# Attention and a gated product on one core: the gate's filter taps, the planner's orders and the split between plain and split matmuls

## The chip, the cores and the metric

The kernel runs on one core of one Trainium2 chip. The metric is the device time of one execution in microseconds (us), the median over runs. A core has five instruction streams here: TensorE (PE, with its weight loads shown as PEld), VectorE (DVE), ScalarE (ACT), GpSimd (POOL), and SyncE (SP), whose queue issues most transfers.

## What is computed

```
B, H, S, D = 8, 12, 448, 64;  DM = 768;  KT = 5
scores = q @ k.T / sqrt(D) - log(S)
attn   = sigmoid(scores)                      # 8 x 12 heads, 448 x 448
x      = attn @ v                             # gathered to (8, 448, 768)
gate   = sigmoid(sum over k of conv_w[k] * x delayed by KT-1-k tokens)   # 5 taps for each channel
out    = (gate * (x @ w_val)) @ w_out
```

Everything is float32 at the interface.

## The kernel before

**Tiles.** Two heads of one batch make a pair: 48 pairs i, six for each batch. Two pairs make a step j, so there are 24 steps, three for each batch. For each pair TensorE makes three chunks of 128 keys of the transposed scores (`scores`, L516), for each step one more accumulator with the remaining 64 keys of both pairs (`scores_rest`, L539), and then the product of the sigmoids with v (`attend`, L602 and L610). All of these use a ring of three PSUM accumulators, `ps_a`. The last step of each batch completes x for 448 tokens. Batch 0's x is written to DRAM and comes back in slices of 64 tokens, one slice behind each of the batches 1 to 7, so the later part works on 7 groups of 512 tokens. For each group, `product` (L753) makes six column blocks of x @ w_val and six of the gated value @ w_out, 18 matmuls of 512 columns each, in a ring of two PSUM accumulators, `ps_m`.

**Two ways to multiply.** A float32 operand can be taken plain, or be split into a high and a low part that are multiplied in three products. `WHOLE` names the steps whose attention product is plain (j from 0 to 7, that is 16 pairs), `WHOLE_SCORES` the pairs whose scores are plain (i from 0 to 14). A plain step needs only a sigmoid on ScalarE for each chunk (`attention`, L552, tile a_single). A split step needs the sigmoid, a scaling on ScalarE (L367, a<-ps_a) and a subtraction on VectorE (L563) for each of its seven accumulators, a maximum over v on VectorE (L531), a one-column matmul for it (L536), four small exponent instructions (L544 to L577) and the two parts of v (L369 or L367, and L583). A split pair needs qk_hi (L361 or L363) and qk_lo, two subtractions on GpSimd (L372).

**The gate.** In `after(j)`, for the groups 1 to 7 (21 steps): x is copied out of PSUM, its maximum taken (L658), and then for each of the step's two channel blocks the first tap is one scaled copy into the gate (L367 or L369). Of the other four taps, the first one or two are multiply-adds on VectorE (L679); the last two (group 1, `ADDED_FIRST`) or three (groups 2 to 7, `ADDED`) are multiplied on ScalarE into a `tap` tile (L367) and added to the gate in memory by a transfer that GpSimd issues (L683). A sigmoid over both blocks follows (L685). The gate is read when a value product leaves PSUM (L777, the tile y), and y then gives the two parts of the operand g of the second product.

**Scale of x.** `x_largest` (L696 to L702) spreads the group's largest |x| over the partitions by two small matmuls, which ride in front of the first chunk of a later pair's scores; `x_scale` and `x_split` then make xs, the operand of the value products.

**Weights.** Each of the twelve column blocks of w_val and w_out is loaded as 64-bit words (L410, a ring of three `words` tiles), converted by a few bit operations (`convert`, L387 to L389, L369 or L367, L412), its maximum taken (L415), and split (L446).

**The order.** No loop of the kernel is the order of the instructions. Each operation is entered in a `Plan` with its engines and modelled costs, a priority, and what it depends on. `issue` runs an event model once and picks for each free engine the ready operation of the lowest priority number. The priorities come from hand-set offsets (`AT`) added to the modelled time `tau` of a pair. An engine then executes its instructions strictly in that order. In the model GpSimd and VectorE don't run at the same time where both operations name "VG" as their port.

Of the kernel before, what the change touches and what calls it, by code (L numbers as in the profile page):

```python
# [10 lines left out]
F32 = mybir.dt.float32  # L11
# [4 lines left out]
U32 = mybir.dt.uint32  # L16
I16 = mybir.dt.int16
I64 = mybir.dt.int64
AF = mybir.ActivationFunctionType
ALU = mybir.AluOpType  # L20
# [18 lines left out]
WHOLE = {*range(8)}  # L39
WHOLE_SCORES = {*range(15)}  # L40
# [15 lines left out]
REBIAS = 2.0**-112  # L56
WN = NC * P
# [5 lines left out]
WORDS = 3  # L63
# [10 lines left out]
ADDED_FIRST = 2  # L74
ADDED = 3
# [3 lines left out]
    first=6.63, step=13.72, val=-77.5, val_step=60.94, out=57.5, out_step=597.15, w_max=-57.5,  # L79
    w_split=-155, load_qk_first=-152, load_qk=69.5, load_v=-40.5, split_hi=-2, split_lo=30,  # L80
    rest_first=95.5, rest=251, a_first=-174.5, a=-7, attend=-47.5, v_max=76.5, v_exp=14.5,
    v_split=-159.5, x=-174.5, x_max=-98, x_scale=-307, x_hi=52.5, x_lo=-185.5, x_step=2940.66, tap=51,
    scores=68.5, a_rest=85, a_rest_first=-72.5, tap_first=22, tap_pair=68.5, tap_step=56.18, gate=-110,
    product=63.5, y=-61.5, g_hi=186.5, g_lo=6, o=-97, share=0.3, w_load=-117,
# [39 lines left out]
class Op:  # L124
    __slots__ = ("ways", "prio", "emit", "deps", "n", "start", "end", "eng", "after", "size", "port", "then")
# [7 lines left out]
class Plan:  # L133
# [45 lines left out]
    def issue(self):  # L179
# [24 lines left out]
        while events:  # L204
# [6 lines left out]
            for e in engines:  # L211
# [24 lines left out]
                if o.size:  # L236
                    bus = max(bus, t + cost) + o.size / self.DMA_RATE
                    o.end = bus + self.DMA_DELAY
                else:
                    o.end = t + cost  # L240
# [3 lines left out]
                for x in nexts[o.n]:  # L244
                    same = e in x.ways and len(x.ways) == 1 and not o.size
                    release(x, o.end + (0.03 if same else self.HOP[e]))
# [6 lines left out]
        return order  # L253


@with_exitstack
def attention_then_gate(
# [51 lines left out]
    gate_ring = ring(sb, 4, [P, 2, T], F32, "gate")  # L309
# [9 lines left out]
    tap_ring = ring(sb, 2, [P, 2, T], F32, "tap")  # L319
# [61 lines left out]
    def convert(w, t, prio, c):  # L381

        low, high = (lambda: w()[:, :, 0]), (lambda: w()[:, :, 1])
        part = lambda n: w().bitcast(I16)[:, :, n]
        op({"V": 0.06 + 0.41 * c}, prio, lambda e: nc.vector.tensor_scalar(  # L387
            low(), low().bitcast(U32), 2.0**-29, 7.0, op0=ALU.mult, op1=ALU.min), [], [t])
        op({"V": 0.06 + 0.76 * c}, prio + 0.1, lambda e: nc.vector.tensor_scalar(  # L389
            part(1), part(3), -0x8000, None, op0=ALU.bitwise_and), [], [t])  # L390
        op({"A": 0.06 + 0.76 * c, "V": 0.06 + 0.41 * c}, prio + 0.2, lambda e: scaled(
            e, high().bitcast(F32), high().bitcast(F32), REBIAS), [], [t])

# [235 lines left out]
    def after(j):  # L629
# [34 lines left out]
        g, at, added = gate_ring.new(), t + AT["tap"], ADDED_FIRST if f == 1 else ADDED  # L664
        for p in range(2):
            st[2 * j + p]["g"] = g
        parts = [lambda p=p: by(g()[:, p, :]) for p in range(2)]
        w = lambda p, k: cw()[:, 2 * c + p, KT - 1 - k : KT - k]
        for p, part in enumerate(parts):
            op({"A": 0.61, "V": 0.41}, at + AT["tap_pair"] * p, lambda e, p=p, part=part: scaled(  # L670
                e, part(), x()[:, p, :, HALO:], w(p, 0)), [x, own, cw], [g])
        for k in range(1, KT):
            tap = tap_ring.new() if k > KT - 1 - added else None
            for p, part in enumerate(parts):
                if tap:
                    op({"A": 0.61}, at + AT["tap_step"] * k - AT["tap_first"] + AT["tap_pair"] * p, lambda e, p=p, k=k, tap=tap: scaled(
                        e, by(tap()[:, p, :]), x()[:, p, :, HALO - k : HALO + SL - k], w(p, k)), [x, own, edge, cw], [tap])
                else:
                    op({"V": 0.67}, at + AT["tap_step"] * k + AT["tap_pair"] * p, lambda e, p=p, part=part, k=k: nc.vector.scalar_tensor_tensor(  # L679
                        part(), x()[:, p, :, HALO - k : HALO + SL - k], w(p, k), part(), op0=ALU.mult, op1=ALU.add),  # L680
                       [x, own, edge, cw], [g])
            if tap:
                op({"G": 1.1}, at + AT["tap_step"] * k, lambda e, tap=tap: nc.gpsimd.dma_start(  # L683
                    g(), tap(), accum_op=ALU.add), [tap], [g], 4 * P * T * 4, "")
        op({"A": 0.95}, t + AT["gate"], lambda e: nc.scalar.activation(g(), g(), AF.Sigmoid), [], [g])  # L685
# [52 lines left out]
    def product(n, b, m):  # L738
# [34 lines left out]
        if n == "val":  # L773
# [4 lines left out]
                y(), po(), y_scale()[:, m : m + 1], gate()[:, m % 2, :], op0=ALU.mult, op1=ALU.mult), [po, gate, y_scale], [y], port="")  # L778
# [38 lines left out]
    def score(i, after=None, sums=(), then=()):  # L817
        first, middle, last = (scores(i, c, sums if c == 0 else ()) for c in range(3))
# [4 lines left out]
        for f in then:  # L823
            f(st[i]["ps", 0])
# [14 lines left out]
    for j in range(TWOS):  # L839
# [18 lines left out]
        if j + 1 < TWOS:  # L858
# [12 lines left out]
            score(2 * j + 3, None, sums, then)  # L871
# [76 lines left out]
```

## Time and profile before

| | us |
|---|---|
| median of 3 runs (578.79 to 579.93) | 579.44 |
| the profiled execution | 579.76 |
| its span, first to last instruction | 578.0 |
| PE busy | 571.4 |
| DVE busy | 428.4 |
| ACT busy | 435.4 |
| POOL busy | 138.2 |

The profile is one execution. Busy time of an engine counts a stretch once where two of its instructions overlap. The time of an execution is the span plus what lies around it, here 1.76 us.

### The profile page before, as it was taken

Reading aid. Unit: us, or ns where it says so; the run is one execution under the profiler, and the core shown is the slowest. Engines: PE = TensorE matmul, PEld = TensorE weight load, DVE = VectorE, ACT = ScalarE, POOL = GpSimd, SP = SyncE. Lnnn points to the kernel's source line nnn. Section 1 sums busy time; section 2 is a strip of 40 time slices with the busy share of each in tenths; the row PEclk is TensorE's granted clock in tenths of the full one; section 3 lists DMA queues with packets and bytes.
Section 4 is the critical chain, followed back from the end, with each engine's and each line's share of the span. In section 5 each row is a group of like instructions: output and inputs, shape, how many; then the busy total and the mean of one; then the engine's idle time right before and its main releaser. Section 6 shows DMA issues by size and latency. Waiting matters only on the chain.

```text
span 578.0 us, 9459 instructions
## 1 busy us (share of the span) xinstructions
PE 571.4 (99%) x3592; PEld 280.2 (48%) x3592; DVE 428.4 (74%) x693; ACT 435.4 (75%) x579; POOL 138.2 (24%) x162
## 2 busy tenths in 40 slices
PE   9999999999999999999999999999999999999997
PEld 5343334455555555545555454554545555544444
DVE  1867999899977959888598886889777886760310
ACT  5677988879888869778697878788788897862112
POOL 0000203332424222243322333223322322110000
PEclk9999999999999999999999999999999999999999
DMA  8988677757484564825657364565635663355012
GB/s 327 355 279 267 174 210 188 203 120 184 124 215 83 146 157 141 207 58 155 136 158 176 102 169 96 166 156 155 169 74 168 155 133 74 72 128 129 2 37 74
DMA packets 39310, 88.44 MB, mean 153 GB/s; under 512 B 14944, under 2 KB 20448, under 8 KB 39264
## 3 DMA queue, kind: packets, MB, share of 16 engines
q0 software_dynamic: 8640, 31.46, 29.4%
q1 hardware_dynamic: 30624, 56.37, 28.9%
q8 instruction: 28, 0.46, 0.3%
q14 instruction: 18, 0.15, 0.1%
HBM read 43.96 MB, written 12.40 MB: 98 GB/s over the span
## 4 chain that ended last, share of the span: by engine, by line
PE 90%; DVE 5%; ACT 3%; DMA 1%; issue 1%; ACTq 0%; DVEq 0%
PE ps_m L753 54%; PE ps_a L516 15%; PE ps_a L610 14%; PE ps_a L539 3%; PE ps_a L602 2%; DMA gate<-tap 1%; ACT a_single L552 1%; DVE x_max L658 1%; DVE gate L679 1%; PE ps_m L800 1%; DVE a L563 1%; DVE w_words L389 1%; DVE out_max L415 0%; ACT tap L367 0%; ACT a L367 0%
## 5 line engine op out<-in xcount | busy, mean ns | idle before, releaser
L753 PE MATMUL ps_m<-g,w_out_hi 128*128 128x512 f16 (+1 forms) x516 | 150.5, 374 | 0.0
L753 PE MATMUL ps_m<-xs,w_val_hi 128*128 128x512 f16 x504 | 150.1, 379 | 0.0
L552 ACT ACTIVATE ps_a<-ps_a 128x896 f32<-128x896 f32 x112 | 99.3, 909 | 14.2 <-DVE v_exp L544 6.5
L563 DVE SCALAR_TENSOR_TENSOR a<-ps_a,a 128x896 f16<-128x896 f32 x96 | 100.8, 1082 | 7.0 <-ACT a L367 6.7
L372 POOL TENSOR_TENSOR qk_lo<-qk_src,qk_hi 128x448 fp32r<-128x448 f32 x66 | 75.2, 1151 | 119.8 <-ACT qk_hi L361 36.7
L753 PE MATMUL ps_m<-g,w_out_lo 128*128 128x512 f16 (+1 forms) x258 | 96.5, 374 | 0.0
L683 POOL DMA_DIRECT2D gate<-tap x60 | 53.5, 892 | 178.6 <-ACT tap L367 70.2
L753 PE MATMUL ps_m<-xs,w_val_lo 128*128 128x512 f16 x252 | 95.5, 379 | 0.0
L367 ACT ACTIVATE a<-ps_a 128x896 f16<-128x896 f32 x96 | 85.0, 927 | 0.2
L367 ACT ACTIVATE tap<-x,cw 128x512 f32<-128x512 f32 x120 | 82.2, 739 | 1.5 <-DMA gate<-tap 1.5
L753 PEld LDWEIGHTS <-w_out_hi 128*128 128x128 f16 x516 | 49.0, 98 | 59.6 <-issue 5.3
L753 PEld LDWEIGHTS <-w_val_hi 128*128 128x128 f16 x504 | 47.8, 98 | 61.1 <-issue 5.9
L777 DVE SCALAR_TENSOR_TENSOR y<-ps_m,y_scale,gate 128x512 f32<-128x512 f32 x42 | 29.9, 745 | 34.3 <-PE ps_m L753 34.3
L610 PE MATMUL ps_a<-a,v_hi 128*64 128x448 f16 x384 | 52.7, 354 | 0.0
L367 ACT ACTIVATE y<-ps_m,o_scale 128x512 f32<-128x512 f32 (+1 forms) x35 | 23.1, 678 | 38.0 <-PE ps_m L753 25.4
L552 ACT ACTIVATE a_single<-ps_a 128x896 f32<-128x896 f32 x56 | 48.0, 927 | 4.5 <-PE ps_a L516 4.1
L361 ACT CAST g<-y 128x512 f16<-128x512 f32 x28 | 17.2, 618 | 33.7 <-DVE y L777 32.9
L516 PE MATMUL ps_a<-qk_hi 64*128 64x448 f32 x198 | 39.8, 398 | 0.1
L753 PEld LDWEIGHTS <-w_out_lo 128*128 128x128 f16 x258 | 25.2, 98 | 29.2
L753 PEld LDWEIGHTS <-w_val_lo 128*128 128x128 f16 x252 | 24.7, 98 | 29.7
L516 PE MATMUL ps_a<-qk_single 64*128 64x448 f32 x180 | 39.0, 566 | 0.0
L610 PE MATMUL ps_a<-a_single,v_src 128*64 128x448 f32 x192 | 37.8, 543 | 0.0
(108 smaller groups left out, 752.9 us busy)
## 6 DMA issues: line engine op xcount, KB each, us to landing
gate<-tap POOLq DMA_DIRECT2D x60, 512.0 KB, 4.9
qk_src<-qk SPq DMA_DIRECT2D x33, 448.0 KB, 5.4
v_src<-vs SPq DMA_DIRECT2D x24, 448.0 KB, 4.3
out_t<-y SPq DMA_DIRECT2D x41, 224.0 KB, 3.1
qk_single<-qk SPq DMA_DIRECT2D x15, 448.0 KB, 5.9
w_words<-w_val SPq DMA_DIRECT2D x6, 768.0 KB, 8.1
w_words<-w_out SPq DMA_DIRECT2D x6, 768.0 KB, 5.4
x<-first_x SPq DMA_DIRECT2D x21, 68.0 KB, 4.2
```

The costliest lines, as they stand in the source:

```text
L361: nc.scalar.copy(to, x)
L367: nc.scalar.activation(to, x, AF.Copy, scale=by)
L372: engines[eng].tensor_tensor(to, x, y, op=ALU.subtract)
L516: mm(b()[:, h, :S], k()[rows, at : at + P], q()[rows, :S], start=(n == 0), stop=(n == len(terms(i)) - 1))
L539: mm(b()[to, h, :S], x[n]()[rows, CW:], x[n]()[rows, :S], start=True, stop=True)
L552: nc.scalar.activation(to, b()[:, :, :S], AF.Sigmoid, bias=-math.log(S), scale=1.0 / math.sqrt(D))
L563: op({"V": 1.0}, t + 0.5, lambda e: nc.vector.scalar_tensor_tensor(part(1), p(), A_SCALE, part(0), op0=ALU.mult, op1=ALU.subtract), [b], [ ...
L602: mm(px()[to, p, :S], v()[rows, h * D : (h + 1) * D], x(s["a"])[rows, h, at : at + S], start=(j > 0 and n == 0), stop=(j == 0 and n == len ...
L610: mm(px()[to, p, :S], v()[:, o : o + D], x(st[2 * j + p]["a", c])[:, h, at : at + S], start=(j == 0 and c == 0 and n == 0), stop=(j > 0 an ...
L683: op({"G": 1.1}, at + AT["tap_step"] * k, lambda e, tap=tap: nc.gpsimd.dma_start(g(), tap(), accum_op=ALU.add), [tap], [g], 4 * P * T * 4, "")
L753: mm(po()[:, cs], w()[:, c, :], x(k)[:, cs], start=(c == 0 and j == 0), stop=(c == NC - 1 and j == 2))
L777: op({"V": 0.66}, t + AT["y"], lambda e: nc.vector.scalar_tensor_tensor(y(), po(), y_scale()[:, m : m + 1], gate()[:, m % 2, :], op0=ALU.m ...
```

## The change

All four later taps become multiply-adds on VectorE, the `tap` tiles and the adding transfers go, and the gate is one tile for each channel block, each with a sigmoid of its own. `WHOLE` loses step 7 (14 pairs remain), `WHOLE_SCORES` pair 14. The ring of weight words has four tiles for three. The first bit operation of a weight's conversion may also go to ScalarE. For step 5 the spreading matmuls ride in front of the third chunk of a pair's scores, not the first. `issue` makes the order four times: after each, `deadlines` walks the order backward from the times at which TensorE's operations would run without a gap and gives every operation of another engine a due time, which is its priority in the next. Of the four orders the one that ends first in the model is used. The hand-set offsets are new numbers.

```diff
-WHOLE = {*range(8)}
-WHOLE_SCORES = {*range(15)}
+WHOLE = {*range(7)}
+WHOLE_SCORES = {*range(14)}
-WORDS = 3
+WORDS = 4
-ADDED_FIRST = 2
-ADDED = 3
+TIMES = 4
...
+    def issue(self):
+        best = None
+        for n in range(TIMES):
+            order = self.order()
+            end = max(o.start + o.ways[o.eng] for o in order)
+            if best is None or end < best[0]:
+                best = end, [(o, o.eng, o.start, o.end) for o in order]
+            self.deadlines(order)
...
+    def deadlines(self, order):
...
+        for o in order:
+            if o.eng == "P":
+                due[o.n] = t = max(t, 0.0)
+                t += o.ways["P"]
+        last = t
+        for o in reversed(order):
+            cost = min(o.ways.values()) + (o.size / self.DMA_RATE + self.DMA_DELAY if o.size else 0.0)
+            at = due.get(o.n, last)
+            for x in nexts[o.n]:
+                at = min(at, x.due - (0.0 if o in (x.after or ()) else cost + self.HOP[o.eng]))
+            o.due = at
+        for o in order:
+            if o.eng != "P":
+                o.prio = o.due
...
-    gate_ring = ring(sb, 4, [P, 2, T], F32, "gate")
+    gate_ring = ring(sb, 8, [P, T], F32, "gate")
-    tap_ring = ring(sb, 2, [P, 2, T], F32, "tap")
...
-        op({"V": 0.06 + 0.41 * c}, prio, lambda e: nc.vector.tensor_scalar(
-            low(), low().bitcast(U32), 2.0**-29, 7.0, op0=ALU.mult, op1=ALU.min), [], [t])
+        op({"V": 0.06 + 0.41 * c, "A": 0.1 + 0.7 * c} if w is not cw_words else {"V": 0.1}, prio, lambda e: nc.vector.tensor_scalar(
+            low(), low().bitcast(U32), 2.0**-29, 7.0, op0=ALU.mult, op1=ALU.min) if e == "V" else scaled(
+            e, low(), w().bitcast(U16)[:, :, 1], TO_THREE_BITS), [], [t])
...
-            if tap:
-                op({"G": 1.1}, at + AT["tap_step"] * k, lambda e, tap=tap: nc.gpsimd.dma_start(
-                    g(), tap(), accum_op=ALU.add), [tap], [g], 4 * P * T * 4, "")
-        op({"A": 0.95}, t + AT["gate"], lambda e: nc.scalar.activation(g(), g(), AF.Sigmoid), [], [g])
+            g = st[2 * j + p]["g"] = gate_ring.new()
+            op({"A": 0.61, "V": 0.41}, at, lambda e, p=p, g=g, w=w: scaled(
+                e, by(g()), x()[:, p, :, HALO:], w(0)), [x, own, cw], [g])
+            for k in range(1, KT):
+                op({"V": 0.67}, at + AT["tap_step"] * k, lambda e, p=p, g=g, w=w, k=k: nc.vector.scalar_tensor_tensor(
+                    by(g()), x()[:, p, :, HALO - k : HALO + SL - k], w(k), by(g()), op0=ALU.mult, op1=ALU.add),
+                   [x, own, edge, cw], [g])
+            op({"A": 0.55}, t + AT["gate"] + AT["tap_pair"] * p, lambda e, g=g: nc.scalar.activation(
+                g(), g(), AF.Sigmoid), [], [g])
...
-            score(2 * j + 3, None, sums, then)
+            score(2 * j + 3, None, sums, then, 2 if j == 5 else 0)
```

## Rows read from the trace of the kernel before

**Rows 1.** The page's first part, the whole span: busy us of each engine with its share of the span and its count of instructions.
```profile
span 578.0 us, 9459 instructions
PE 571.4 (99%) x3592; PEld 280.2 (48%) x3592; DVE 428.4 (74%) x693; ACT 435.4 (75%) x579; POOL 138.2 (24%) x162
```

**Rows 2.** The waits of TensorE: who waited for whom, us in total, times, longest.
```profile
PE ps_m L800 <- DVE ones L793: 1.1, 1, 1.1
PE ps_a L702 <- ACT diagonal L367: 0.9, 1, 0.9
PE ps_a L539 <- ACT a_single L552: 0.7, 2, 0.4
```

**Rows 3.** The chain of work that ended last, in order of time: start us, us, what. A plain pair's scores, a plain step's attention product (two rows), a split step's (two rows), a split pair's scores, the last run of products.
```profile
31.29 2.46 PE ps_a L516 x12
...
109.42 0.75 PE ps_a L602 x8
110.18 4.66 PE ps_a L610 x24
...
409.20 0.57 PE ps_a L602 x12
409.77 3.52 PE ps_a L610 x36
413.29 2.03 PE ps_a L516 x18
...
510.72 63.52 PE ps_m L753 x312
```

**Rows 4.** TensorE's instructions in order of time: start us, us, engine, line, operation, tiles, form, count, and in brackets the idle time before and what ended it.
```profile
78.51 0.22 PE L702 MATMUL ps_a<-diagonal,ones 128*128 128x64 bf16 x2 [0.91 <-ACT diagonal L367]
...
108.34 0.17 PE L536 MATMUL ps_a<-vm,ones 128*128 128x1 bf16 x1
108.44 0.98 PE L539 MATMUL ps_a<-qk_src 64*64 64x448 f32 x8
```

**Rows 5.** Busy time in four stretches: the stretch, its length, then us busy (and instructions) of PE, PEld, DVE, ACT and POOL, the granted clock, the share of the DMA engines, GB/s.
```profile
20.00:60.00 40.00, 39.66 (x233) 15.06 (x233) 29.89 (x64) 30.64 (x38) 0.92 (x3) 1.00 0.84 281
60.00:140.00 80.00, 78.69 (x468) 34.81 (x464) 76.68 (x136) 68.86 (x94) 22.09 (x24) 1.00 0.70 170
140.00:507.00 367.00, 366.89 (x2455) 188.88 (x2451) 296.50 (x455) 303.55 (x405) 110.87 (x121) 1.00 0.57 140
507.00:578.00 71.00, 67.22 (x333) 31.97 (x329) 18.61 (x30) 20.74 (x30) 3.42 (x4) 1.00 0.29 75
```

**Rows 6.** Groups of instructions by line and form over the whole span: line, engine, operation, tiles, shapes, count, then us busy, mean ns of one, idle us before them and what ended it.
```profile
L367 ACT ACTIVATE tap<-x,cw 128x512 f32<-128x512 f32 x120 | 82.2, 739 | 1.5 <-DMA gate<-tap 1.5
L683 POOL DMA_DIRECT2D gate<-tap x60 | 53.5, 892 | 178.6 <-ACT tap L367 70.2 <-DVE gate L679 29.6 <-ACT y L367 21.5
...
L679 DVE SCALAR_TENSOR_TENSOR gate<-x,cw,gate 128x512 f32<-128x512 f32 x48 | 36.0, 763 | 0.0
...
L685 ACT ACTIVATE gate<-gate 128x1024 f32<-128x1024 f32 x21 | 22.4, 1066 | 1.1 <-DMA gate<-tap 1.1
...
L583 DVE SCALAR_TENSOR_TENSOR v_lo<-v_src,v_exp,v_hi 128x896 f16<-128x896 f32 x16 | 18.4, 1151 | 2.0 <-ACT v_hi L367 0.4
L563 DVE SCALAR_TENSOR_TENSOR a_rest<-ps_a,a_rest 128x896 f16<-128x896 f32 x16 | 17.5, 1091 | 21.5 <-ACT a_rest L367 21.5
L531 DVE TENSOR_REDUCE vm<-v_src 128x1 bf16<-128x896 f32 x16 | 17.3, 1079 | 0.0
...
L573 DVE TENSOR_SCALAR v_exp<-v_exp 128x1 int32<-128x1 int32 x16 | 2.5, 153 | 0.5
```

**Rows 7.** The instructions that touch the tile tap, in one stretch: length, us busy (and instructions) of ACT and POOL, clock, DMA share, GB/s.
```profile
40.00:140.00 100.00, 16.60 (x24) 10.56 (x11) 1.00 0.72 187
```

**Rows 8.** VectorE's instructions in order of time, columns as in rows 4: two taps back to back, two subtractions back to back, the first y of group 2 (the seventh and eighth of all), and the low part of g.
```profile
74.45 1.39 DVE L679 SCALAR_TENSOR_TENSOR gate<-x,cw,gate 128x512 f32<-128x512 f32 x2
...
118.79 2.08 DVE L563 SCALAR_TENSOR_TENSOR a<-ps_a,a 128x896 f16<-128x896 f32 x2
...
174.75 1.40 DVE L777 SCALAR_TENSOR_TENSOR y<-ps_m,y_scale,gate 128x512 f32<-128x512 f32 x2
...
251.79 0.68 DVE L372 TENSOR_TENSOR g<-y,g 128x512 f16<-128x512 f32 x1
```

**Rows 9.** ScalarE's instructions in order of time: four taps back to back, two scalings back to back.
```profile
59.76 2.61 ACT L367 ACTIVATE tap<-x,cw 128x512 f32<-128x512 f32 x4
...
117.32 1.73 ACT L367 ACTIVATE a<-ps_a 128x896 f16<-128x896 f32 x2
```

**Rows 10.** The instructions that touch a tile of weight words, in one stretch: length, us busy (and instructions) of DVE and ACT, clock, DMA share, GB/s.
```profile
60.00:140.00 80.00, 29.60 (x32) 4.86 (x5) 1.00 0.70 170
```

**Rows 11.** The waits of the SP queue for a free tile of weight words: who waited for whom, us in total, times, longest.
```profile
SPq L410 <- DVE w_val_lo L446: 7.7, 5, 2.5
```

**Rows 12.** GpSimd's instructions in order of time, columns as in rows 4: one subtraction of 448 columns, and one of the same form that starts while the last instruction of rows 8 runs.
```profile
230.38 1.13 POOL L372 TENSOR_TENSOR qk_lo<-qk_src,qk_hi 128x448 fp32r<-128x448 f32 x1 [1.36 <-ACT qk_hi L361]
...
251.96 1.50 POOL L372 TENSOR_TENSOR qk_lo<-qk_src,qk_hi 128x448 fp32r<-128x448 f32 x1 [2.01 <-DVE qk_hi L363]
```

**Rows 13.** The instructions of L363 (first row) and of L369 (second row) in one stretch: copies and scalings that the planner may give to VectorE or to ScalarE. Length, us busy (and instructions) of VectorE, clock, DMA share, GB/s.
```profile
140.00:507.00 367.00, 26.76 (x52) 1.00 0.57 140
...
140.00:507.00 367.00, 31.16 (x50) 1.00 0.57 140
```

## What was predicted

> **What bounds the kernel now.** I read the page's first part first: TensorE is busy for 571.4 of 578.0 us, VectorE and ScalarE for about three quarters [rows 1]. A busy TensorE need not be the bound, so next came its waits: three kinds, 2.7 us together, and 1.1 of that is the start [rows 2]. The chain of waits ends in TensorE's own products: their last run ends at 510.72 + 63.52 = 574.24, with 3.8 us of copying and storing behind it [rows 3]. The stretches then show where it was close. From 140 to 507 us TensorE is busy for 366.89 of 367.00 us; from 60 to 140 it loses 1.3 us, and there VectorE is busy for 76.68 of 80 us and ScalarE for 68.86 [rows 5]. So the time is TensorE's instruction stream, plus 1.6 us of waits between 40 and 90 us, plus both ends. The granted clock is 1.00 in all four stretches, its upper level of 2.4 GHz [rows 5]. Two things can move the time: what TensorE has to do, and whether the other engines still keep it fed.
>
> **TensorE's work.** Step 7 becomes a split step. A plain step's attention product takes 0.75 + 4.66 = 5.41 us of TensorE, a split one 0.57 + 3.52 = 4.09 [rows 3]: 1.32 us less. Pair 14's scores go from 2.46 to 2.03 us: 0.43 less [rows 3]. A split step adds a one-column matmul, which holds the next back by 108.44 - 108.34 = 0.10 us [rows 4]. Net: 1.65 us less, all of it on the path, since TensorE has no slack to hide it in.
>
> **The wait at 78 us.** TensorE waits 0.91 us there, in front of the spreading matmuls, for ScalarE's diagonal [rows 2, 4]. The change puts these matmuls, for this group alone, in front of the third chunk of the scores. Two chunks are two thirds of 2.46, or 1.64 us of work in between [rows 3], more than the wait. I take the 0.91 as gained. Between nothing and 0.91 I take the upper end because the work put in between exceeds the wait. Behind the matmuls that may still wait stand the third chunk, the rest accumulator and the attention product of the next step on TensorE, and ScalarE waits for their results; late next is a sigmoid: the other 0.7 us are waits for one, and I leave them [rows 2].
>
> **The taps.** Sixty transfers, 120 taps on ScalarE and 53.5 us of issuing on GpSimd go [rows 6]. A tap on ScalarE costs 2.61/4 = 0.65 us from start to start [rows 9]. Each becomes a tap on VectorE at 1.39/2 = 0.70 us [rows 8]. TensorE has no wait for a load or for one of these transfers [rows 2], so the freed transfer engines and the freed GpSimd queue give nothing directly. Twenty-one sigmoids of 1024 columns become 42 of 512: at worst as long as a tap of 512 columns, 42 x 0.74 = 31.1 us for 22.4 [rows 6], at best no longer than now. That is at most 9 us of ScalarE spread over some 450 us, and ScalarE is the less loaded engine after the change; I take zero. Eight half-width gate tiles hold what four did.
>
> **60 to 140 us.** This is the narrow place, so I count the load of VectorE and ScalarE together. Now it is 76.68 + 68.86 = 145.5 of 160 us, so 14.5 are idle [rows 5].
> - ScalarE's 24 taps and 11 transfers up to 140 us [rows 7] go: 24 x 0.65 = 15.6 less. On VectorE they come back as 24 x 0.70 = 16.8.
> - Step 7 split: on VectorE seven subtractions at 2.08/2 = 1.04 [rows 8], a maximum 1.08, the low part of v 1.15, four small ones at 0.15 [rows 6]: 10.1. On ScalarE seven scalings at 1.73/2 = 0.87 and the high part of v, about as much: 6.9 [rows 9].
> - Sum: 16.8 + 10.1 + 6.9 - 15.6 = 18.2 more, against 14.5 idle. It doesn't fit as it stands.
> - Relief one: 12 of the 24 taps, and 4 more that VectorE does now, belong to group 2, whose first y is made at 174.75 [rows 8]. A due time puts them behind what TensorE needs sooner: 16 x 0.70 = 11.2 leave the stretch.
> - Relief two: between 20 and 60 us VectorE and ScalarE are idle for 10.1 and 9.4 us [rows 5], partly because the load of a weight waits for one of three tiles, 7.7 us in all [rows 11]. With four tiles about one weight can come earlier. The six output weights cost 29.60 + 4.86 us in the stretch [rows 10], some 5.7 each. On SP's queue that load (128 x 768 x 8 bytes, 2.8 us at 281 GB/s [rows 5]) then stands ahead of loads of pairs and of v; TensorE waits for none of these now [rows 2], so I take nothing for it, at worst 2.8 us once.
> - Left: 18.2 - 11.2 - 5.7 = 1.3 us. I take this as hidden in the 14.5 us of idle time. If that cover fails, TensorE waits about half of what is left over, since two engines share it: 0.7 us. With no relief it would be 9.1.
>
> **140 to 507 us.** VectorE has 296.5 us now. The 90 taps left to this stretch (120 less 24, and 6 in the tail) and the 16 postponed make 63 + 11.2 more: 371, over the 367 that there are [rows 5]. But 26.8 + 31.2 = 58 us of it are copies and scalings that ScalarE may do [rows 13], and ScalarE has lost 58.5 of 303.6. Moved as a whole VectorE falls to 313; half of them moved gives 342. So VectorE will be at 85 to 93% where it was at 81%, and ScalarE lower. VectorE does wait now in every step (21.5 us in front of the 16 rests alone, [rows 6]), so I take no wait of TensorE, against up to 0.35 us for each of 15 steps, half a tap that stands in front of a subtraction.
>
> **Tail.** TensorE has products ready from 507 us on, and VectorE is busy for 18.61 of 71 us [rows 5]; six more taps change nothing.
>
> **Sum.** The profiled execution took 579.76 us, 0.32 above the median of 579.44. 579.76 - 1.65 - 0.91 = 577.20; the same step from the median gives **576.9**.
>
> **Rivals.**
> - *Gain lost between 60 and 140 us, no measurable change.* For it: that stretch is almost full now. If no weight comes earlier, 7.0 us are left over, and TensorE waits 1.8 (half of that absorbed) to 3.5 us: 578.7 to 580.4.
> - *VectorE late there, slower.* The same place, with half of the reliefs: 18.2 - 8.4 = 9.8 us, TensorE waits 4.9 and the time is 581.8; with none, 586.0. It is slower from 2 x (2.56 + 1.16) = 7.4 us of unabsorbed work on. The gates of group 1 are then late, y holds one of the two product accumulators, and TensorE stands before the next product. Against it: due times exist to put such work first, and the idle time of the stretch before.
> - *Taps in the way, step after step.* VectorE executes in order; 0.35 us in each of 15 steps is 5.2 us: 582.1. Against it are the waits of VectorE itself.
> - *Taps against GpSimd.* A subtraction that starts at 251.96 while VectorE makes the low part of g, from two operands in SBUF, takes 1.50 us, where one alone takes 1.13 [rows 8, 12]. A tap too reads x and the gate. If one subtraction in each of 15 steps were pushed by 0.37 us and TensorE waited for it, that would be 5.6 us: 582.5. GpSimd is busy for 110.87 of 367 us [rows 5] and loses its transfers, so I give it little. The Trainium skill, SBUF — State Buffer, section "Who interferes with whom", states this as a rule: a VectorE instruction with two SBUF inputs and a GpSimd instruction that reads SBUF exclude each other, and the one that comes second waits. By that rule every one of the 120 added taps can hold up a subtraction, or be held up by one; the trace agrees, with its 0.37 us, that the second comer waits.
> - *The due times don't take effect.* If the first of the four orders is kept, only the offsets are new; the matmuls still go, the wait at 78 us may stay: 577.8.
>
> **Chances.** Forecast 0.55; due times without effect 0.03, also faster. No measurable change 0.19. Late between 60 and 140 us 0.12, taps in the way 0.07, taps against GpSimd 0.04. A measurement of this kernel can tell about 0.2%, 1.16 us, from no change: faster ends at 578.3, slower begins at 580.6. So faster 0.58, same 0.19, slower 0.23. The range: downward all of the waits of [rows 2] but the start gone, 579.44 - 1.65 - 1.6 = 576.2, and the 0.65 us by which the lowest run lies below the median: 575.5. Upward to the first slower case, 581.8; beyond it are the other two slower rivals and the worst end of this one, under 2 in 10. The likeliest case alone lies between 575.5 and 578.3.
>
> **What would show it.** In the changed profile: no transfers on GpSimd's queue but no more waits of TensorE than now; 168 taps on VectorE at about 0.75 us each; no wait for the diagonal at 78 us; TensorE busy some 569.8 us; VectorE some 490 to 520 us of 575 (428.4 + 84 + 10.1, less what moves to ScalarE), ScalarE below its 435.4. Wrong would be: a wait of TensorE for VectorE's y, subtraction or rest, of more than 1 us in sum, or TensorE idle between 60 and 140 us for more than now. A step between 140 and 507 us that takes longer than now would speak for the last two slower rivals.

## The result and the profile after

The changed kernel takes **585.0 us** (median, 584.46 to 585.48) where the kernel before takes 579.46 (578.79 to 579.93): a ratio of 1.0098, interval 1.0086 to 1.011. It is 5.5 us slower, against a forecast of 2.5 us faster. Of the 8.1 us between, by the starts of the attention products, about 2.8 were lost before step 8 at 135 us, 4.7 in the steady part and 0.7 at the end. (The 2.8 is rough: the first attention product starts anywhere from 9.8 to 11.2 us in the profiles of this case, and 0.3 us later here than in the kernel before.) The profiled execution took 585.48 us, its span is 583.7.

The lines of the change moved: the taps are L713 (L679 before), the gate's sigmoids L716, scores L558, rest L581, attention products L644 and L652, sigmoids of scores L594, subtractions L605, value and output products L785, the scaling by a factor L408 on ScalarE and L410 on VectorE, GpSimd's subtraction L413.

The page's first part answers to [rows 1].

```profile
span 583.7 us, 9415 instructions
...
PE 572.9 (98%) x3615; PEld 281.3 (48%) x3615; DVE 489.8 (84%) x794; ACT 392.4 (67%) x516; POOL 100.7 (17%) x110
```

Load went where it was said to go: VectorE 61 us up, ScalarE 43 down. The waits of TensorE answer to [rows 2] (who waited for whom, us, times, longest).

```profile
PE ps_a L558 <- DVE a_rest L605: 2.2, 5, 0.6
PE ps_a L558 <- ACT a_single L594: 1.3, 1, 1.3
PE ps_m L832 <- DVE ones L825: 1.1, 1, 1.1
PE ps_a L581 <- ACT a_single L594: 0.5, 1, 0.5
PE ps_a L558 <- ACT x_first L402: 0.5, 1, 0.5
PE ps_a L558 <- DVE v_exp L619: 0.3, 1, 0.3
```

The wait for the diagonal is gone. New are five waits for a buffer of scores that VectorE's subtraction of the rest part (`a_rest`) still holds, and one of 1.3 us for a sigmoid. The stretches answer to [rows 5], with the same columns.

```profile
20.00:60.00 40.00, 39.04 (x231) 14.82 (x229) 35.82 (x73) 32.46 (x40) 0.32 (x3) 1.00 0.86 300
60.00:140.00 80.00, 78.36 (x495) 36.56 (x493) 79.28 (x135) 64.00 (x87) 20.95 (x18) 1.00 0.28 89
140.00:507.00 367.00, 364.29 (x2403) 186.13 (x2404) 346.55 (x546) 262.86 (x346) 75.11 (x75) 1.00 0.25 75
```

VectorE is full from 60 to 140 us (79.28 of 80) and at 94% after it; TensorE loses 2.7 us between 140 and 507, where it lost 0.1. The loss is larger than this idle time, since short stalls lie within matmuls: the attention product of step 8 starts 0.2 us later than before, that of the last step 4.96 (508.75 against 503.79). The clock stays at 1.00. Where in time it is lost, the chain shows. The attention products of the kernel before (start us, us, what):

```profile
360.06 3.53 PE ps_a L610 x36
...
434.59 3.52 PE ps_a L610 x36
...
484.29 3.53 PE ps_a L610 x36
...
503.79 3.53 PE ps_a L610 x36
```

The same four steps after the change:

```profile
363.38 3.54 PE ps_a L652 x36
...
438.72 3.54 PE ps_a L652 x36
...
489.26 3.53 PE ps_a L652 x36
...
508.75 3.53 PE ps_a L652 x36
```

From the first to the second it was 74.53 us and is 75.34: 0.81 us lost in three steps, one group. From the second to the third (two steps) it was 49.70 and is 50.54: 0.84 lost there already, and in the last step, 19.50 to 19.49, nothing. So the loss goes by groups, 0.8 to 1.2 us in each, and not by steps. The place is the step in which the group's x is scaled into xs. One such place, all engines in order of time (columns as in [rows 4]):

```profile
304.71 0.35 DVE L404 CAST qk_hi<-qk_src 128x384 fp32r<-128x384 f32 x1
304.80 2.65 POOL L413 TENSOR_TENSOR qk_lo<-qk_src,qk_hi 128x448 fp32r<-128x448 f32 x2 [7.02 <-DVE x_exp L443]
304.97 1.63 DVE L410 TENSOR_SCALAR xs<-x,x_exp 128x1024 f16<-128x1024 f32 x1
...
311.54 0.98 PE L581 MATMUL ps_a<-qk_src 64*64 64x448 f32 x8
...
311.91 1.27 DVE L764 SCALAR_TENSOR_TENSOR xs<-x,x_exp,xs 128x1024 f16<-128x1024 f32 x1
313.10 0.74 DVE L713 SCALAR_TENSOR_TENSOR gate<-x,cw,gate 128x512 f32<-128x512 f32 x1
...
313.77 0.14 DVE L586 TENSOR_SCALAR v_exp<-ps_a 128x1 int32<-128x1 int32 x1
...
313.87 0.63 ACT L716 ACTIVATE gate<-gate 128x512 f32<-128x512 f32 x1 [1.54 <-DVE gate L713]
314.41 0.90 ACT L594 ACTIVATE ps_a<-ps_a 128x896 f32<-128x896 f32 x1
...
315.76 0.90 ACT L408 ACTIVATE a_rest<-ps_a 128x896 f16<-128x896 f32 x1
...
316.69 1.09 DVE L605 SCALAR_TENSOR_TENSOR a_rest<-ps_a,a_rest 128x896 f16<-128x896 f32 x1 [1.68 <-ACT a_rest L408]
...
317.83 0.47 PE L558 MATMUL ps_a<-qk_hi 64*128 64x448 f32 x2 [0.42 <-DVE a_rest L605]
```

Read it from below. TensorE waits for the subtraction at 316.69, that for ScalarE's scaling, that for the sigmoid of the rest part at 314.41. TensorE had made this sigmoid's input by 312.5 (311.54 + 0.98), but ScalarE works in order and stood for 1.54 us before a gate's sigmoid, whose last tap came at 313.10. The sigmoid also has to wait for `v_exp`, which reads the same accumulator and comes behind the same tap, at 313.77. VectorE came to this tap late: it was busy without a break from the scaling at 304.97 on, and this scaling took 1.63 us. The shortest such scaling takes 0.75. This one started 0.17 us after GpSimd's subtraction.

Groups of instructions by line and form (columns as in [rows 6]):

```profile
L713 DVE SCALAR_TENSOR_TENSOR gate<-x,cw,gate 128x512 f32<-128x512 f32 x168 | 121.4, 755 | 1.9 <-DVE x L703 0.9
...
L410 DVE TENSOR_SCALAR xs<-x,x_exp 128x1024 f16<-128x1024 f32 x8 | 11.7, 1476 | 0.0
L716 ACT ACTIVATE gate<-gate 128x512 f32<-128x512 f32 x42 | 26.3, 631 | 19.1 <-DVE gate L713 19.0
L408 ACT ACTIVATE w_words<-w_words 128x768 f32<-128x768 f32 x8 | 7.4, 924 | 7.0 <-DVE w_words L431 6.2 <-DVE y_scale L501 0.7
```

Seven of the eight scalings of x ran beside a subtraction of GpSimd that had begun first, and all seven took 1.46 to 1.63 us: 5.8 us of VectorE more than at 0.75 each. ScalarE stands idle for 19 us before the gates' sigmoids, where it was 1.1 [rows 6], and for 7 us before conversions of weights. The second sum is not new: the kernel before waits 8.2 us for VectorE there, at places where TensorE has other work. In the early loss such a wait stands in front of sigmoids that TensorE wants (here and in TensorE's row, columns as above):

```profile
63.77 0.97 ACT L408 ACTIVATE w_words<-w_words 128x768 f32<-128x768 f32 x1 [2.71 <-DVE w_words L431]
...
66.71 0.92 ACT L408 ACTIVATE w_words<-w_words 128x768 f32<-128x768 f32 x1 [0.67 <-DVE w_words L431]
67.53 4.93 ACT L594 ACTIVATE a_single<-ps_a 128x896 f32<-128x896 f32 x6
```

```profile
68.48 2.63 PE L558 MATMUL ps_a<-qk_single 64*128 64x448 f32 x12 [1.29 <-ACT a_single L594]
```

### The profile page after: what moved, and what is told of

Read it like the earlier page. It is cut to its first block, busy times and chain, and to the rows that moved or that the text cites. A ratio compares the mean times of both kernels' runs of the same rounds, so it can differ in the third digit from the quotient of the medians.

```text
span 583.7 us, 9415 instructions
## 1 busy us (share of the span) xinstructions
PE 572.9 (98%) x3615; PEld 281.3 (48%) x3615; DVE 489.8 (84%) x794; ACT 392.4 (67%) x516; POOL 100.7 (17%) x110
## 4 chain that ended last, share of the span: by engine, by line
PE 52%; DVE 33%; ACT 9%; issue 4%; DMA 2%; SPq 0%; DVEq 0%; ACTq 0%
PE ps_m L785 32%; PE ps_a L558 9%; DVE a L605 8%; PE ps_a L652 7%; DVE gate L713 6%; DVE xs L764 3%; ACT a_single L594 2%; ACT ps_a L594 2%; PE ps_a L581 2%; DVE xs L410 2%; DVE qk_hi L404 1%; DVE a_rest L605 1%; DVE v_lo L625 1%; PE ps_a L644 1%; DVE vm L573 1%
## 5 line engine op out<-in xcount | busy, mean ns | idle before, releaser
L785 PE MATMUL ps_m<-g,w_out_hi 128*128 128x512 f16 (+1 forms) x516 | 150.6, 374 | 0.2 <-ACT y L408 0.2
L785 PE MATMUL ps_m<-xs,w_val_hi 128*128 128x512 f16 x504 | 150.1, 379 | 0.0
L413 POOL TENSOR_TENSOR qk_lo<-qk_src,qk_hi 128x448 fp32r<-128x448 f32 x68 | 81.3, 1212 | 279.1 <-DVE qk_hi L404 124.1
L713 DVE SCALAR_TENSOR_TENSOR gate<-x,cw,gate 128x512 f32<-128x512 f32 x168 | 121.4, 755 | 1.9 <-DVE x L703 0.9
L594 ACT ACTIVATE ps_a<-ps_a 128x896 f32<-128x896 f32 x119 | 105.8, 907 | 10.0 <-DVE v_exp L586 6.0
L605 DVE SCALAR_TENSOR_TENSOR a<-ps_a,a 128x896 f16<-128x896 f32 x102 | 106.8, 1080 | 3.7 <-ACT a L408 3.7
L785 PE MATMUL ps_m<-g,w_out_lo 128*128 128x512 f16 (+1 forms) x258 | 96.5, 374 | 0.0
L785 PE MATMUL ps_m<-xs,w_val_lo 128*128 128x512 f16 x252 | 95.5, 379 | 0.0
L408 ACT ACTIVATE a<-ps_a 128x896 f16<-128x896 f32 x102 | 89.9, 924 | 0.2
L785 PEld LDWEIGHTS <-w_out_hi 128*128 128x128 f16 x516 | 49.0, 98 | 59.9 <-issue 5.6
L785 PEld LDWEIGHTS <-w_val_hi 128*128 128x128 f16 x504 | 47.9, 98 | 60.8 <-issue 5.5
L402 ACT CAST g<-y 128x512 f16<-128x512 f32 x34 | 21.1, 620 | 73.6 <-DVE y L809 73.3
L408 ACT ACTIVATE y<-ps_m,o_scale 128x512 f32<-128x512 f32 (+1 forms) x40 | 26.3, 679 | 51.1 <-PE ps_m L785 40.1
L652 PE MATMUL ps_a<-a,v_hi 128*64 128x448 f16 x408 | 56.0, 355 | 0.0
L594 ACT ACTIVATE a_single<-ps_a 128x896 f32<-128x896 f32 x49 | 41.8, 925 | 6.9 <-PE ps_a L558 4.1
L558 PE MATMUL ps_a<-qk_hi 64*128 64x448 f32 x204 | 42.3, 411 | 2.9 <-DVE a_rest L605 2.2
L785 PEld LDWEIGHTS <-w_out_lo 128*128 128x128 f16 x258 | 25.2, 98 | 29.2
L716 ACT ACTIVATE gate<-gate 128x512 f32<-128x512 f32 x42 | 26.3, 631 | 19.1 <-DVE gate L713 19.0
L785 PEld LDWEIGHTS <-w_val_lo 128*128 128x128 f16 x252 | 24.7, 98 | 29.7
L558 PE MATMUL ps_a<-qk_single 64*128 64x448 f32 x168 | 36.6, 569 | 1.7 <-ACT a_single L594 1.3
L558 PE MATMUL ps_a<-qk_hi,qk_lo 64*128 64x448 f32 x204 | 37.3, 362 | 0.0
```

The costliest lines, as they stand in the source:

```text
L402: nc.scalar.copy(to, x)
L408: nc.scalar.activation(to, x, AF.Copy, scale=by)
L413: engines[eng].tensor_tensor(to, x, y, op=ALU.subtract)
L558: mm(b()[:, h, :S], k()[rows, at : at + P], q()[rows, :S], start=(n == 0), stop=(n == len(terms(i)) - 1))
L594: nc.scalar.activation(to, b()[:, :, :S], AF.Sigmoid, bias=-math.log(S), scale=1.0 / math.sqrt(D))
L605: op({"V": 1.0}, t + 0.5, lambda e: nc.vector.scalar_tensor_tensor(part(1), p(), A_SCALE, part(0), op0=ALU.mult, op1=ALU.subtract), [b], [ ...
```

## The experiments

The changed kernel and then four groups of runs (rows 2 to 5, 6 to 9, 10 to 12, and 13 of the table) were each timed beside the kernel before, each group on one chip. The kernel before took 579.17 to 579.50 us there, so a difference between two groups is sure to about 0.3 us only.

| kernel | us | ratio to before (95%) |
|---|---|---|
| changed | 585.0 | 1.0098 (1.0086 to 1.011) |
| due_only | 584.83 | 1.0093 (1.0076 to 1.0109) |
| half_taps | 579.14 | 0.9995 (0.9986 to 1.0005) |
| const_exp | 585.03 | 1.0091 (1.0076 to 1.0106) |
| no_weight_wait | 583.41 | 1.0066 (1.0051 to 1.0081) |
| gate_apart | 583.34 | 1.0062 (1.0049 to 1.0075) |
| split_first | 581.33 | 1.0029 (1.0019 to 1.0039) |
| all_three | 579.46 | 1.0002 (0.9993 to 1.001) |
| pairs16 | 585.54 | 1.01 (1.0085 to 1.0116) |
| share05 | 579.81 | 1.001 (1.0001 to 1.0019) |
| replanned | 579.13 | 0.9997 (0.9988 to 1.0006) |
| share05_split | 580.36 | 1.002 (1.0011 to 1.0029) |
| replanned16 | 577.38 | 0.9965 (0.9951 to 0.9979) |

**due_only**, the kernel before with the order of the first pass of due times and nothing else of the change (the change's `issue` and `deadlines` go in whole; its choice of an order is fixed to the second):

```diff
-            if best is None or end < best[0]:
+            if n == 1:
```

> The kernel before with the order made after one pass of due times, and nothing else of the change: taps on ScalarE and by transfers, 16 plain pairs, three weight tiles, old offsets. Theory O (an order by due times is planned without slack, so that what TensorE needs stands behind work that was begun just before it): slower than before by 2 to 4 us, 581.5 to 583.5, with new waits of TensorE for VectorE and ScalarE. Theory L (168 taps fill VectorE, and any order would wait): within 1 us of before, 578.5 to 580.5.

584.83 us, more than either theory gave. The profile shows one event, not a steady loss: TensorE is busy for all 367 us from 140 on, and the waits show

```profile
PE ps_a L744 <- ACT diagonal L409: 3.1, 1, 3.1
```

So due times alone do not make the steady part late, and with these offsets they make the early part worse: the wait that the change removed grew from 0.9 to 3.1 us. It costs more than its length: TensorE stands idle for 3.08 us, and then from 82 to 84 and from 84 to 86 us its granted clock is 0.60 and 0.55, near its lower level of 1.2 GHz, where it is 1.00 before and after. A plain pair's scores take 3.85 us there, for 2.46 [rows 3]. The kernel's own event model ends this order 3.0 us later than the first one, so the change's rule would not have kept it; the run tells of due times, not of that rule. Four of the scalings of x that VectorE makes here from 140 us on take 1.62 to 1.63 us beside GpSimd, and TensorE loses nothing by it.

**half_taps**, the changed kernel in its own order, each tap on four of the eight segments of x:

```diff
-                    by(g()), x()[:, p, :, HALO - k : HALO + SL - k], w(k), by(g()), ...
+                    by(g())[:, :4], x()[:, p, :4, HALO - k : HALO + SL - k], w(k), by(g())[:, :4], ...
```

> The kernel after, the same order on every engine, but each of the four later taps works on half of its 512 columns (the other half of the gate keeps the first tap only). VectorE loses about 0.3 us at each of 168 places, 50 us in all. Theory L: nearly all of TensorE's new waits go, 579 to 580. Theory O: the chains behind the taps come earlier, but those waits that start at an in-order wait between ScalarE and VectorE stay: 581.5 to 583.5.

579.14 us, 5.9 less. A tap takes 492 ns for 755, and the waits of the steady part are gone:

```profile
140.00:507.00 367.00, 367.00 (x2447) 188.47 (x2446) 315.63 (x545) 264.77 (x349) 74.69 (x75) 1.00 0.24 73
```

VectorE's time in that order is what the loss hangs on. The scalings of x still take 1491 ns here, as seven of the eight still run beside GpSimd, so with enough idle time on VectorE they cost nothing. Whether the load has to be cut, or only put elsewhere, this run can't tell.

**const_exp**, `v_exp` reads a constant, so the sigmoid of the rest part does not wait for VectorE's small operation:

```diff
-            e()[:, :1], b()[:, 0, S : S + 1].bitcast(I32), 0x7F800000, ...
+            e()[:, :1], quarter().bitcast(I32), 0x7F800000, ...
```

> The kernel after, the same order, but the first exponent instruction of a split step (L586) reads a constant in SBUF, not the maximum in PSUM, so that the sigmoid of the rest accumulator does not wait for VectorE to come to it; the maximum over v is left out of the scale. The load of every engine is the same. Theory O: the rest's chain (exponent, sigmoid, scaling, subtraction) starts up to 1.3 us earlier in the steps where TensorE waits, and most of its 4.0 us of waits after 140 us go: 581.5 to 582.5. Theory L: nothing is lighter, so 584.5 to 585.5.

585.03 us, no change: that wait alone is not it. As gate_apart shows below, it stands behind another one.

**no_weight_wait**, ScalarE's conversions of weights work on tiles of their own:

```diff
-            e, high().bitcast(F32), high().bitcast(F32), REBIAS), [], [t])
+            e, unused(), other().bitcast(F32), REBIAS), [], [t])    # on ScalarE only
```

> The kernel after, the same order, but where ScalarE does the third step of a weight's conversion it works on tiles of its own, so that it doesn't wait for VectorE in front of the sigmoids (those weights' values are not the real ones). Theory O: of the 2.2 us that TensorE waits between 30 and 70 us for sigmoids behind such a step, 1.5 or more go: 583.0 to 583.6. Theory L: VectorE does the same work, so at most 0.5 us: 584.4 to 585.4.

583.41 us, 1.6 less, and the wait of 1.3 us at 68 us is gone. This part of the loss is the waiting between ScalarE and VectorE at conversions. The run does not part its two directions: VectorE's next step of such a weight reads a tile of its own too, and with that 3.7 us go that VectorE stood there for ScalarE in the changed kernel. That it is ScalarE's wait that counts is read from the trace alone.

**gate_apart**, **split_first** and **all_three** take the steady loss apart.

```diff
-                g(), g(), AF.Sigmoid), [], [g])
+                apart(), apart(), AF.Sigmoid), [], [g])          # gate_apart
...
+                while last_split:                                 # split_first, before each qk_lo
+                    nc.gpsimd.tensor_copy(after_split(), last_split.pop()()[:, 0, :1])
```

> The changed kernel with its order unchanged; ScalarE's 42 gate sigmoids (L716) work on a tile of their own, so that they wait for no tap of VectorE (the gate that goes into the product has then no sigmoid). Theory Q (ScalarE's queue: in the changed kernel it stands idle 19 us in front of these sigmoids, and the sigmoid of the scores that TensorE's rest part leaves stands right behind one of them; that makes VectorE's subtraction and so the buffer of scores late): the waits of TensorE between 140 and 507 us go, about 4.5 us, the early ones stay: 580.0 to 581.5. Theory P (the port: VectorE's scalings of x run at half speed beside GpSimd's subtractions, 5.9 us in all, and that makes the subtraction late): little changes, 584 to 585.2. Theory L (VectorE has simply too much to do in that order): as theory P, 584 to 585.2.

> The changed kernel with its order unchanged, but GpSimd copies one element of each scaled x (xs) before its next subtraction (qk_lo), so that this subtraction starts after VectorE's (or ScalarE's) scaling, as the order was planned. Theory P: the scalings on VectorE take 0.74 us for up to 1.63, VectorE is 0.8 to 1.7 us earlier at each of the six rest parts that were late, and the waits between 140 and 507 us shrink from 4.5 us to under 1: 580.5 to 582. Theory Q: VectorE's taps are earlier by the same 0.8 us at most, the sigmoid of the gate follows them at once, so a part of the loss goes: 582 to 584. Theory L: as before, 584 to 585.5, or slower if the later subtraction now makes scores late.

> The three reliefs together, order unchanged: ScalarE's conversions of weights and gate sigmoids on tiles of their own, and GpSimd's subtraction behind the scaling of x. Weights and gates are then not what they should be. If the early 1.6 us of the conversions and the steady 4.5 us are the whole loss and have these causes: 578 to 579.5, the predicted 576.9 plus the two early waits of 0.5 us and the longer end of 0.7 us. If the load itself costs the time, 582 to 583.5, no better than the conversions alone (583.4).

gate_apart takes 583.34 us, 1.7 less: between the two theories. The sigmoid of the rest part no longer stands behind a gate, but at the place shown above it then waits 1.23 us for `v_exp`, which VectorE makes behind the same late tap. Two waits held one instruction, so taking away either (const_exp, gate_apart) showed little. split_first takes 581.33, 3.7 less. It changes only when GpSimd starts, and VectorE's groups and the same place show what that does:

```profile
L412 DVE TENSOR_SCALAR xs<-x,x_exp 128x1024 f16<-128x1024 f32 x8 | 6.7, 850 | 0.0
```

```profile
303.12 0.75 DVE L412 TENSOR_SCALAR xs<-x,x_exp 128x1024 f16<-128x1024 f32 x1
...
303.94 0.19 POOL L539 COPY after_split<-xs 128x1 f16<-128x1 f16 x1 [8.04 <-DVE xs L412]
304.07 2.10 POOL L415 TENSOR_TENSOR qk_lo<-qk_src,qk_hi 128x448 fp32r<-128x448 f32 x2
...
311.34 0.63 ACT L722 ACTIVATE gate<-gate 128x512 f32<-128x512 f32 x1 [0.87 <-DVE gate L719]
```

The scaling takes 0.75 us for 1.63 (of the seven slow ones six are cured; the one near 85 us still takes 1.58 beside a subtraction, hence the mean of 850 ns), the gate's sigmoid waits 0.87 for 1.54, and GpSimd's own subtractions take 2.10 for 2.65. TensorE loses 0.3 us of the 367 for 2.7. So the clash of VectorE and GpSimd is the larger part of the steady loss. Left alone, GpSimd starts as soon as its operand is there; the planner had put the scaling first and nothing held GpSimd to that. all_three takes 579.46: 5.5 less than the changed kernel, less than the sum of the three (6.9), which fits gate and clash acting on one chain. Its steady part is full (367.00 of 367), with VectorE at 343.98 us, hardly less than the 346.55 of the changed kernel.

**pairs16**, the changed kernel with `WHOLE` and `WHOLE_SCORES` back at 8 and 15:

```diff
-WHOLE = {*range(7)}
-WHOLE_SCORES = {*range(14)}
+WHOLE = {*range(8)}
+WHOLE_SCORES = {*range(15)}
```

> The changed kernel with 16 pairs in plain float32 again (7 steps and 14 pairs become 8 and 15), planned anew with the same offsets. TensorE has 1.65 us more to do in the sum of the prediction, in step 7 and the scores of pair 14, both near 85 to 105 us; VectorE and GpSimd are rid of one step's splits there. If the time there is TensorE's: 586 to 587. If VectorE's load there is what bounds: 584 to 585, no slower. If the new order meets other waits, either way by up to 3 us, which tells that the order's luck outweighs the pairs.

585.54 us, not to be told from the changed kernel. The plan was new throughout, with 0.6 us of waiting for the diagonal and 0.9 for `v_exp` that weren't there, so this says little of the pairs.

**share05**, **replanned** and **share05_split** keep every tap on VectorE and change offsets of the planner; share05_split adds GpSimd's copy of split_first to share05.

```diff
-    g_lo=44.5, o=-115, share=0, w_load=-94,
+    g_lo=44.5, o=-115, share=0.5, w_load=-94,
```

> One number of the changed kernel is altered: the planner's share is 0.5 us for 0, so that VectorE leaves an operation that ScalarE may do as well to ScalarE if that is free within 0.5 us. The plan is made anew; by its lists some 20 us of scalings and copies move from VectorE (467 us planned) to ScalarE (382 us), all 168 taps stay on VectorE. Theory W (the loss is waits of the order: the port, ScalarE's queue behind the conversions, the gates): the new order need not meet them, and if it doesn't the time is the predicted 576.9 plus the two early waits of 0.5 us and the longer end of 0.7 us: 577 to 579. Theory L (VectorE's load): taking 41 us of taps away gave 5.9 us, so 20 us give 2.9: 582. If the order's luck decides, any of them may stay: up to 585.

> As share05, with three offsets altered as well (tap_step -51.2 for 11.31, g_lo 20.5 for 44.5, attend 60.1 for -32.5), which changes the first of the four orders and with it the due times. By its lists 24 us move from VectorE to ScalarE. Theory W: 576.5 to 578.5, no wait of TensorE over 0.3 us between 140 and 507 us. Theory L: 581.5 to 582.

> share05 with GpSimd's copy of one element of each scaled x before its next subtraction, as in split_first. If the port still costs in the order of share05, it is 1 to 3 us faster than share05; if that order has no such clash at a place that decides, the same within 0.5 us.

share05: 579.81, 5.2 less by one number, where the load alone would have given 2.9 by the rate of half_taps. In it 16 of the 21 scalings of x are on ScalarE (13 in the changed kernel), and the five on VectorE take 744 ns. replanned: 579.13, 5.9 less; TensorE is busy for 367.00 of 367 with VectorE at 330.88. Both are above what was expected, by 0.8 and 0.6 us: between 20 and 115 us TensorE still waits, 0.9 us for copies of x and 0.9 for sigmoids. share05_split is 0.5 us slower than share05, at the edge of what was expected. None of share05's five scalings on VectorE runs beside a subtraction, so the copy had nothing to cure; why it costs 0.5 us was not traced.

**replanned16** goes back to 16 pairs, with share 0.8 and nine offsets altered:

> All taps on VectorE and due times as in the changed kernel, but 16 pairs in plain float32 again, share 0.8 for 0 and nine offsets altered (val, val_step, w_split, load_qk_first, rest, rest_first, v_exp, tap, scores). Step 7 and pair 14 cost TensorE 1.65 us more than in replanned (579.13), and spare VectorE, ScalarE and GpSimd a step's splits between 60 and 140 us, some 17 us of work. Theory W, carried on: what kept replanned from the predicted 576.9 are its waits between 20 and 115 us, 1.1 us more than in the kernel before, and they come from the load that the split of step 7 adds there; without it TensorE need not wait between 20 and 507 us, and the time is 579.2 less the 1.6 us of waits of the kernel before: 577.3 to 578.3. If the split of step 7 was a gain all the same, this is slower than replanned by up to 1.65: 580.8.

577.38 us, 2.0 less than the kernel before and 7.6 less than the changed one. Its waits and stretches:

```profile
PE ps_m L832 <- DVE ones L825: 1.1, 1, 1.1
PE ps_a L581 <- ACT a_single L594: 0.4, 2, 0.2
PE ps_m L785 <- ACT y L408: 0.2, 1, 0.2
```

```profile
60.00:140.00 80.00, 79.81 (x483) 36.47 (x480) 75.78 (x142) 69.31 (x94) 17.52 (x16) 1.00 0.34 113
140.00:507.00 367.00, 367.00 (x2447) 188.56 (x2446) 329.80 (x494) 285.69 (x392) 64.96 (x69) 1.00 0.23 72
```

All 168 taps are on VectorE, and TensorE waits for nothing that counts. So the taps there need not cost time. Two things have changed together, though: the order, and VectorE's load from 140 to 507 us, 329.80 us for 346.55, as more scalings and copies are on ScalarE. These last runs do not part them; that the load of the changed kernel can be borne is shown by all_three, at 343.98 us in its own order.

## Why the prediction was wrong

- **TensorE's work: right in size.** In the changed kernel the rest matmuls in front of step 7's attention product start at 109.78 and the next scores at 114.79, 5.01 us; before it was 6.33, from 108.44 [rows 4] to 114.77. That is the 1.32 of the sum. TensorE's busy time is 569.8 us in all_three, the number given, and 572.9 in the changed kernel, as short stalls lie within matmuls.
- **The wait at 78 us: right.** It is gone.
- **The taps: the duration right (755 ns), their place in ScalarE's queue missed.** The step priced the 42 sigmoids at zero because ScalarE has time. But ScalarE works in order, and each of these sigmoids waits for a tap with other work behind it: 19 us idle for 1.1, 1.7 us of the end by gate_apart. The idle time itself is not the price: replanned16 has 13.3 us of it, and TensorE waits for nothing that counts.
- **60 to 140 us: the count of the load right, the cover failed.** VectorE and ScalarE come to 79.28 + 64.00 = 143.3 us there, no more than the 145.5 + 1.3 of the count. Relief one held: 24 taps run between 40 and 140 us, as many as it left there. Relief two held as a count: 4.7 us of the weights' work left the stretch (34.46 to 29.78 us), where 5.7 were taken. But "hidden in the idle time" pools two engines: VectorE has 0.7 us of it left and ScalarE 16. The price, put at nothing, lay in ScalarE's queue: a conversion that waits for VectorE's step in front of sigmoids that TensorE wants. no_weight_wait prices that at 1.6 us of the early 2.8; all_three still waits 0.5 and 0.3 us for the rest part's sigmoids and the copy of the first x. Whether the fourth tile or the new order put the conversions there is not shown, as no run kept three tiles; replanned16 has four and does not lose there.
- **140 to 507 us: the step that failed most.** "No wait of TensorE" rested on VectorE's own waits, 21.5 us in front of 16 rests [rows 6]. They show that VectorE is early on the average, not that it is early in the one step of each group where x is scaled. The hand-over to ScalarE fell short as well: 44.7 of the 58 us of copies and scalings stayed on VectorE, which then had 346.55 us, above the 342 counted for half. The sign named for this case came: 2.2 us of waits for the rest's subtraction, against 1. The bound, half a tap in each of 15 steps (5.2 us), was near the measured 4.7, but by luck, as the loss has another form: 0.8 to 1.2 us in each group, at that step. By split_first 3.7 us of it hang on the clash of VectorE and GpSimd there.
- **The rival of taps against GpSimd named the right pair of engines and, where it cost most, the wrong instruction.** [rows 8, 12] showed GpSimd's subtraction held up. The trace after shows VectorE's scaling held up, 7 of 7 beside a subtraction begun before. Seven taps overlap a subtraction too: the three that began second took 2.1 us longer in all, and where the tap began first GpSimd's subtraction was the longer one, as the rival said (1.61 to 1.67 us for 1.16 on three of them). The Trainium skill, SBUF — State Buffer, section "Who interferes with whom", says as well that `tensor_scalar` can run in a mode that takes the port pair shared with GpSimd for the whole instruction, and that the order of issue decides who is blocked. The prediction took from it only the rule on two SBUF inputs. By this one the 12 scalings on VectorE of the kernel before were at risk as well. The trace agrees on both: one of those 12 took 1.62 us there, and subtractions with one operand in PSUM (`a`) overlap GpSimd 53 times in the changed kernel and are never longer.
- **The tail: 0.7 us instead of nothing.** The changed kernel's products after the last attention product end 0.33 us later against it, in part by a wait of 0.2 us for `y`; the other 0.4 of the span lie behind the last matmul. No run was made on it.
- **The range.** Each slower rival was a case by itself, at 581.8 to 582.5 (586.0 for the early one at its worst). Two came true together, one early and one steady, and their losses add up.
- **The due times took effect.** The order that the kernel's own model keeps is the second of the four, the first made by due times, so that rival is out.

What stays open: why all_three is at 579.46 and not at 576.9. Its waits besides the start come to 1.7 us, where the prediction left 0.7. By place: from step 8's attention product to step 11's it takes 75.53 us (132.78 to 208.31) where the kernel before takes 74.86 (135.40 to 210.26), 0.7 lost; its tail is 0.7 longer, as in the changed kernel; and 2.2 us of an execution lie outside the span, for 1.8. That is 1.8 of the 2.5 us; the rest would lie before step 8, where it still waits. None of this was tested. Nor do these runs show what 14 pairs are worth in an order without waits: the best order measured for them takes 579.13, the best for 16 pairs 577.38.

## What to carry to other kernels

When work moves to an engine with idle time on the average, look at the one step in a period where that engine has most to do, and ask what stands behind each wait in the in-order queues of the others. A planned order between two engines that share something holds only if a dependency enforces it: an engine that waits on a semaphore starts when it can, not when the plan says. When a wait is removed and nothing moves, look for a second one on the same instruction before clearing it.

## What the hardware showed

A blocked instruction shows as a longer one, not as idle time: VectorE's scaling of 1024 columns takes 0.75 us alone and 1.46 to 1.63 us when GpSimd's subtraction began 0.2 to 0.5 us before it. One element copied by GpSimd (0.19 us) in front of its subtraction restored the 0.75 in six of seven places (split_first). The order with the clash became 3.7 us faster by it, the order without 0.5 us slower (share05_split). In these runs the clash has a price only where VectorE is short of time: in half_taps seven scalings are slow and TensorE loses nothing.
